# Queries, keys and four gate/up tiles of two token blocks as 2x2 block products of seven, in a layernorm, attention and SwiGLU kernel

## The chip, the cores and the metric

The kernel runs on one core of one Trainium2 chip. The metric is the device time of one execution in microseconds (us). The kernel before was run three times: median 1383.19, from 1383.1 to 1384.01. One further execution was profiled, and all views of the profile and the trace come from it.

## The reference, cut to what matters

```python
S, D, H, F = 2048, 512, 32, 1792           # rows of x, model width, heads (of 16), inner width
x  = A_x                                   # B_x is not used; all of it is fp32
xn = layernorm(x)                          # no scale, no shift
q, k, v = split(xn @ wqkv)                 # wqkv 512 x 1536, 32 heads of 16
s  = concat(softmax(q k^T / 4) v) @ wo     # full attention, no mask
h  = silu(xn @ w_gate) * (xn @ w_up)       # 2048 x 1792
g  = silu(h @ w_down)
out = x + s * g
```

## The kernel before

**Arithmetic.** Nearly all products run as three passes of the format fp32r: each operand is cut into a high part (a cast to fp32r) and a low part (the rest, by a subtract), and high x high, high x low and low x high are added in PSUM. Names ending in h and l, or a pair of tiles of one kind (`wh`/`wl`, `guh`/`gul`, `xt_...` twice), are such high and low parts. Only the product of probabilities and values (L450) runs in plain fp32.

**Blocks.** The 2048 rows are four blocks (b = 0 to 3) of 512 tokens. `xt` holds the normalised rows of a block turned, features on partitions, as high and low part; there are two buffers, so block 2 writes over block 0's and block 3 over block 1's.

**The prologue** runs 48 slots, twelve for each block: four value tiles (`value_tile`) and eight feature tiles (`feature_tile`, four of queries and four of keys, 128 features each). A slot is 12 full matmuls (L723 or L725: four chunks of 128 input features, three passes each). For blocks 0 and 1 the value tiles come first, for blocks 2 and 3 last. Behind the matmuls of a feature tile ScalarE takes the square (L778) and the high part (L779), VectorE the low part (L780), SyncE's queue stores both to `q_d` or `k_d`, and VectorE keeps the elementwise maximum of the squares in `top` (L784). A value tile is copied to `vt` and stored to `v_d` (L788), by GpSimd's queue for blocks 0 to 2.

The work between slots is set by a table of steps, `step(at, late, ...)`: at slot `at`, ahead of (0) or behind (1) its tile. `columns_of(b, ...)` places a block's rows: the load of x, its statistics and rates, a transpose of these (`spread_mr`), their way through DRAM (`mr_d`) into `wide_mr`, a tile with each token's mean and rate on all partitions (`load_mr`, L679, on GpSimd's DMA queue); then VectorE subtracts and multiplies each chunk in place (L667, `raw_x<-raw_x,wide_mr`), ScalarE casts it to the high part, VectorE makes the low part (also L667, `xt<-raw_x,xt`), and `store_x` (L658) stores the block's `xt` to `xt_d`, also on GpSimd's queue. The gate and down products of later blocks read `xt_d` into `fx` again; block 0's `fx` is copied directly (L819).

After the last feature tile the squares are summed by head and give a bound on all scores. Where it is small enough (`flag`), one common shift is used in place of each row's maximum; `tc.If` branches on it (L884, L887), and with these data the general way behind the branch isn't taken.

**The attention** runs 32 units (eight groups of four heads, four blocks of queries), each over 16 tiles of 128 keys. `plan()` cuts each unit into blocks of 2 to 6 key tiles, 102 blocks in all, by a search over costs. A block has two slots for each key tile, each with two score matmuls (L979, two heads side by side in the halves of the array), whose exponentials ScalarE makes from PSUM (L982 for two banks at once, L989 for one); the value matmuls of the block before stand behind the first key tile (L450). Where `SHARED` names slots of a block, VectorE copies one PSUM bank out (L986), and ScalarE exponentiates that copy at the end of the block (L999). L999 runs 354 times.

**The fill.** The rest of the plan says how many steps of other work follow each slot, so that TensorE has work while ScalarE makes exponentials. A step is a pair of matmuls on the two halves of the array (`both`, L244), which add into two banks. The steps come from a queue: `ffn(b)` for b = 0 to 3 in turn, each with inner tiles in two halves of seven; a half is seven gate units of 24 steps (gate and up together; their weights are cut by `split_gu`, L205 and L206) and four down units of 21 steps. `th` is the tanh of silu, `ga` the gated tile, `hh` its high and low part, `wd` those of w_down's tile, `facc` the sum of the first half of a block. Behind them comes the output projection, `project_out`, in part in the last units. The first 24 of these steps stand before the branch:

```python
                    fill(3 * DC)
                    fast = nc.values_load(flag, min_val=0, max_val=1)
```

Two value tiles' matmuls, the last slots of the prologue, are queued behind the reading of the flag as well, as the order below shows. L410 and L442, named in the prediction, are the closing sums of the output (GpSimd and VectorE); L579 is 11 matmuls of zeros at the very start, L639 the transposes of block 0's rows, L1034 the last products.

## Time and profile before

| | us |
|---|---|
| median of three runs | 1383.19 (1383.1 to 1384.01) |
| span of the profiled execution | 1381.3 |
| TensorE, matmuls busy | 1374.6 |
| TensorE, weight loads busy (beside matmuls) | 868.4 |
| ScalarE busy | 1157.9 |
| VectorE busy | 780.3 |
| GpSimd busy | 105.2 |
| DMA | 156.29 MB in 132900 packets |

The profile lists no time of the profiled execution but its span, which lies 1.9 us below the median of the other three runs. Busy times of different engines overlap. Half-height matmuls run in pairs, so the sum of their durations is more than the time that they fill, and a group of them reads 0.39 us for one while a pair takes 0.23.

### The profile page before, as it was taken

What the parts mean: (1) busy time and instruction counts of PE and PEld (TensorE: products, weight loads), DVE (VectorE), ACT (ScalarE), POOL (GpSimd) and SP (SyncE); (2) the same over time, 40 slices, a digit from 0 to 9 for tenths busy, and PEclk for the clock granted to TensorE, in tenths of its full rate; (3) what the DMA queues carried; (4) which work ended last, traced back from release to release, by engine and by line L of the source; (5) the groups of instructions that cost most, each with busy time, mean ns of one, the idle gap of its engine ahead of it and who ended that gap; (6) DMA issues with size and microseconds to landing.
All of it is one profiled execution on the core that took longest, in us unless ns stands there. A gap on an engine that the chain in (4) does not pass through costs nothing.

```text
span 1381.3 us, 27646 instructions
## 1 busy us (share of the span) xinstructions
PE 1374.6 (100%) x11152; PEld 868.4 (63%) x11152; DVE 780.3 (56%) x1255; ACT 1157.9 (84%) x1944; POOL 105.2 (8%) x148
## 2 busy tenths in 40 slices
PE   9999999999999999999999999999999999999998
PEld 7887666666655665665556656566556556656565
DVE  7674465356555663565465644565466445655656
ACT  6753689888988888899998998888989888899875
POOL 4300100000010000000010000000100000000142
PEclk9999999999999999999999999999999999999999
DMA  9799531134553511133814402257323312234652
GB/s 302 256 353 283 140 93 43 43 78 97 123 116 82 135 44 36 51 98 87 175 49 110 112 13 51 74 128 153 82 70 89 99 28 54 60 87 137 217 191 84
DMA packets 132900, 156.29 MB, mean 113 GB/s; under 512 B 13481, under 2 KB 83137, under 8 KB 131998
## 3 DMA queue, kind: packets, MB, share of 16 engines
q1 hardware_dynamic: 124974, 128.03, 36.0%
q0 software_dynamic: 7312, 25.89, 5.5%
q8 instruction: 89, 1.46, 0.5%
q10 hardware_dynamic: 480, 0.54, 0.1%
q14 instruction: 45, 0.37, 0.1%
HBM read 112.18 MB, written 40.12 MB: 110 GB/s over the span
## 4 chain that ended last, share of the span: by engine, by line
PE 89%; DVE 0%; DVEq 0%; issue 0%
PE acc L450 33%; PE bankx L244 29%; PE score L979 10%; PE single L979 8%; PE banky L244 7%; PE spare L979 1%; PE spare L1034 0%; PE banky L1034 0%; PE single L1034 0%; DVE guh L205 0%; DVE y L1041 0%; PE score L1034 0%; DVE y L1047 0%; DVEq L1094 0%; DVEq L205 0%
## 5 line engine op out<-in xcount | busy, mean ns | idle before, releaser
L450 PE MATMUL acc<-pr,vst 128*17 128x512 f32 x4096 | 459.3, 593 | 0.0
L989 ACT ACTIVATE pr<-single 128x512 f32<-128x512 f32 x762 | 429.5, 605 | 17.1 <-PE single L979 0.5
L982 ACT ACTIVATE pr<-score 128x1024 f32<-128x1024 f32 x318 | 328.1, 1032 | 87.1 <-PE score L979 84.3
L450 PEld LDWEIGHTS acc<-pr,vst 128*17 128x17 f32 x4096 | 115.5, 97 | 279.5 <-issue 275.2
L244 PE MATMUL banky<-fx,guh 64*128 64x512 f32 x896 | 291.0, 392 | 0.0
L244 PE MATMUL bankx<-fx,guh 64*128 64x512 f32 x896 | 290.6, 391 | 0.1
L986 DVE COPY pr<-spare 128x512 f32<-128x512 f32 x194 | 134.2, 692 | 182.7 <-PE spare L979 168.3
L979 PE MATMUL score<-qst,kst 50*128 50x512 f32 x830 | 219.0, 417 | 0.0
L979 PE MATMUL single<-qst,kst 50*128 50x512 f32 x922 | 212.7, 398 | 0.0
L244 PE MATMUL bankx<-wd,hh 64*128 64x512 f32 x672 | 196.0, 391 | 0.0
L244 PE MATMUL banky<-wd,hh 64*128 64x512 f32 x672 | 196.0, 391 | 0.0
L999 ACT ACTIVATE pr<-pr 128x512 f32<-128x512 f32 x354 | 193.4, 642 | 0.0
L244 PEld LDWEIGHTS bankx<-fx,guh 64*128 64x128 f32 x896 | 166.8, 186 | 21.0 <-DVE guh L205 0.5
L244 PE MATMUL bankx<-fx,gul 64*128 64x512 f32 x448 | 175.5, 392 | 0.0
L244 PE MATMUL banky<-fx,gul 64*128 64x512 f32 x448 | 175.5, 392 | 0.0
L979 PEld LDWEIGHTS score<-qst,kst 50*128 50x128 f32 x830 | 98.9, 183 | 112.4 <-ACT pr L989 69.0
L244 PEld LDWEIGHTS banky<-fx,guh 64*128 64x128 f32 x896 | 166.9, 186 | 0.7
L989 ACT ACTIVATE pr<-score 128x512 f32<-128x512 f32 x194 | 116.9, 603 | 35.5 <-PE spare L979 28.0
L986 DVE COPY pr<-single 128x512 f32<-128x512 f32 x160 | 110.5, 691 | 59.6 <-PE single L979 44.6
L244 PEld LDWEIGHTS bankx<-wd,hh 64*128 64x128 f32 x672 | 125.1, 186 | 16.4
L979 PEld LDWEIGHTS single<-qst,kst 50*128 50x128 f32 x922 | 115.0, 184 | 23.1 <-ACT pr L989 7.6
L244 PEld LDWEIGHTS banky<-wd,hh 64*128 64x128 f32 x672 | 125.1, 186 | 6.8
(195 smaller groups left out, 1690.1 us busy)
## 6 DMA issues: line engine op xcount, KB each, us to landing
gur<-in_B_w_gate_dram SPq DMA_DIRECT2D x56, 256.0 KB
gur<-in_B_w_up_dram SPq DMA_DIRECT2D x56, 256.0 KB
wdr<-in_B_w_down_dram SPq DMA_DIRECT2D x56, 256.0 KB
kst<-k_d SPq DMA_DIRECT2D x192, 64.0 KB
qst<-q_d SPq DMA_DIRECT2D x192, 64.0 KB
fx<-xt_d SPq DMA_DIRECT2D x24, 512.0 KB
q_d<-parts SPq DMA_DIRECT2D x16, 512.0 KB
k_d<-parts SPq DMA_DIRECT2D x16, 512.0 KB
```

The source lines that it names most:

```text
L244: mm(bank, lhs[h], rhs[h], start=start, stop=stop)
L450: mm(acc[h * 32:h * 32 + DH + 1], v[:, kt % CT, h * (DH + 1):(h + 1) * (DH + 1)], probs[2 * i + h // 2][:, h % 2], start=kt == 0, stop=kt ...
L979: mm(banked[h], k[r, j, kc * P:(kc + 1) * P], q[r, j], start=True, stop=True)
L982: exps.append(act(pr, both_banks, AF.Exp, scale=0.25))
L986: dve.tensor_copy(pr[:, h], banked[h])
L989: exps.append(act(pr[:, h], banked[h], AF.Exp, scale=0.25))
L999: exps.append(act(part, part, AF.Exp, scale=0.25))
```

## The change

**Seven products.** Queries and keys of blocks 2 and 3, and four of the 14 inner tiles of gate and up (`AHEAD`) for the same blocks, are computed in the prologue as eight jobs. A job takes two 128-wide tiles of weights (a query or key pair, or up and gate of one inner tile) against the two blocks of tokens, and reads them as a 2x2 product of blocks, split in the halves of the 512 input features: seven products in place of eight, by sums of weights and sums of rows. The 16 feature tiles of blocks 2 and 3 leave the slots, so that 32 slots are left: 12, 12, 4 and 4. Behind slot 31 come the jobs (q/k pair 0, pair 2, tile 0, pair 1, tile 1, pair 3, tile 7, tile 8), each of 7 x 6 full matmuls (L963).

A job's banks: the first and third product add up in one bank, which ScalarE copies after the first (`m1`, L972); VectorE adds the second to it (`w`, L974), and the fifth to that (`u3`, L988); `c12` (L999) and `c21` (L1005) are made by VectorE from the sixth and seventh, `c22` by GpSimd from `u3` and `m5`, ScalarE's copy of the fourth. The rows' sums are made once, from slot 26 on (`split_turn`, L908, cuts them in parts `twh`/`twl` that lie where weights were); the weights' sums on GpSimd (`sums`, L913 to L916), cut by `whole_of` and `summed_of` (L923 to L938) during the job before. Behind a q/k job's four results come square, high part, low part, store and maximum as before, with c22's low part on GpSimd; a gate/up job makes tanh and products `g1`, `g2` and stores them to `h_d`.

**Block 3 comes 8 slots earlier**, since eight feature tiles have gone ahead of it. Its rows are loaded into `facc` (called `xin`) and not `raw_x`, where GpSimd's sums now go.

**The branch.** The flag is made during the last job, and read behind it; no fill steps stand before the branch, and no value tile behind the reading.

**The FFN** runs by halves over `SEQUENCE`: half 0 of blocks 0, 2, 3, half 1 of blocks 0, 2, 3, 1, and half 0 of block 1, so that w_down's half is loaded three times and not eight. The sums of a first half of blocks 2 and 3 wait in `p_d`. The gated tiles made ahead come back from `h_d` into `hh` (`load_hidden`) and are cut by `split_hidden`. Gate steps fall from 56 units to 48.

**The plan** has new costs and 106 blocks, `SHARED` new entries (such copies rise from 354 to 422), and the value matmuls of a block take its tiles with shared slots last.

```diff
+AHEAD = (0, 1, 7, 8)
+    for b, grp in ((0, 0), (2, 0), (3, 0), (0, 1), (2, 1), (3, 1), (1, 1), (1, 0)):
...
-    short = lambda k, n: 60 if (k, n) in SHARED else 250 * max(0, 6 * (k - 1) - n)
+    short = lambda k, n: WAIT[k] + (65 if k == 4 else 160) * max(0, ENOUGH[k] - n)
...
+    def load_hidden(b, grp):
+        for f in AHEAD:
+            if b > 1 and GROUPS[grp].start <= f < GROUPS[grp].stop:
+                hidden.append(f - GROUPS[grp].start)
+                sp.dma_start(hh[:, hidden[-1], 1].bitcast(F32), h_d[b - 2, f])
...
-        u, tiles, probs = item
-        for i, kt in enumerate(tiles):
+        u, tiles, probs, order = item
+        for at, i in enumerate(order):
...
-    columns_of(2, raw_x, raw_x, (4, 11, 7, 9, 13, 13, 19, (1, 2, 3, 3)))
-    columns_of(3, xin, raw_x, (18, 24, 23, 25, 27, 27, 31, (1, 2, 3, 3)))
+    columns_of(2, raw_x, raw_x, (4, 11, 7, 9, 13, 13, 19, ((0, 0, 1), (1, 1, 2), (2, 2, 3), (3, 3, 3))))
+    columns_of(3, xin, xin, (14, 18, 16, 18, 20, 22, 24, ((0, 0, 1), (0, 1, 2), (1, 1, 2), (1, 2, 3))))
...
+        def split_turn(i, src):
+            t = turns_x[i] = [pc.tile([P, 2, TB], F32R, tag=f"{n}{i}", name=f"t{n}{i}") for n in ("wh", "wl")]
+            nc.scalar.copy(t[0], src)
+            dve.tensor_sub(t[1], src, t[0].bitcast(F32))
+
+        def sums(i):
+            s = raw_x.rearrange("p (i c) t -> p i (c t)", i=2)[:, i % 2].rearrange("p (i f) -> p i f", i=4)
+            raw = raws[i]
+            pool.tensor_add(s[:, 0], raw[:, 0], raw[:, 1])
+            pool.tensor_sub(s[:, 1], s[:, 0], raw[:, 2])
+            pool.tensor_sub(s[:, 2], raw[:, 2], raw[:, 0])
+            pool.tensor_sub(s[:, 3], raw[:, 3], s[:, 1])
...
+            if more:
+                sums(i + 1)
+            product(bank[0], whole[1], b11, True, False)
+            nc.scalar.copy(m1, bank[0])
+            product(bank[1], summed[1], t2, True, True)
+            dve.tensor_add(w, bank[1], m1)
+            if more:
+                whole_of(i + 1)
+            product(bank[0], whole[2], b21, False, True)
...
+                feature_out(2 * f, 2, bank[0], False)
+            product(bank[2], summed[0], t1, True, False)
+            nc.scalar.copy(m5, bank[2])
+            if between:
+                between()
+            product(bank[3], summed[2], t3, True, False)
+            dve.tensor_add(u3, bank[3], w)
+            pool.tensor_add(c22, u3, m5)
+            if more:
+                summed_of(i + 1)
...
+            product(bank[2], summed[3], b22, False, True)
+            dve.tensor_add(c12, bank[2], w)
...
+                feature_out(2 * f, 3, c12, False)
+            product(bank[3], whole[0], t4, False, True)
+            dve.tensor_add(c21, bank[3], w)
...
+                feature_out(2 * f + 1, 3, c22, True)
+                feature_out(2 * f + 1, 2, c21, False)
+
+        lower_x, upper_x = xin[:, :2], xin[:, 2:]
+        b11, b21 = ([xt[0][j][:, 2 * h:2 * h + 2].bitcast(F32) for j in range(2)] for h in range(2))
+        step(26, 1, dve.tensor_sub, wide_mr, upper_x, lower_x)
+        for j in range(2):
+            step(27, j, dve.tensor_sub, lower_x, lower_x, b11[j])
+        step(28, 0, dve.tensor_sub, upper_x, upper_x, lower_x)
+        step(28, 1, split_turn, 0, upper_x)
+        step(29, 0, split_turn, 1, lower_x)
+        step(29, 1, split_turn, 2, wide_mr)
+        step(30, 0, dve.tensor_sub, wide_mr, b21[0], upper_x)
+        step(30, 0, dve.tensor_add, wide_mr, wide_mr, b21[1])
+        step(30, 1, split_turn, 3, wide_mr)
+        step(26, 1, sums, 0)
...
-                    fill(3 * DC)
-                    fast = nc.values_load(flag, min_val=0, max_val=1)
...
+        for i in range(len(jobs)):
+            strassen(i, {6: bound, 7: spread_shift}.get(i))
+        load_wd(0, 0)
+        fast = nc.values_load(flag, min_val=0, max_val=1)
```

In the new program the stores of `store_x` are L719, `load_mr` is L740, the chunks' work L728, a feature tile's maximum L847, the flag L1098 and the branch L1100.

GpSimd's queue from block 1's store of values on, before (in these rows, `xt_169` and `xt_170` are block 2's, `xt_171` and `xt_172` block 3's high and low parts):

```order
L788 DMA v_d<-vt 128x8x272
L658 DMA xt_d<-xt_169 128x2048
L658 DMA xt_d<-xt_170 128x2048
L679 DMA wide_mr<-mr_d 128x1024
L658 DMA xt_d<-xt_171 128x2048
L658 DMA xt_d<-xt_172 128x2048
```

The same place in the new program (block 2 has `xt_177` and `xt_178`, block 3 `xt_179` and `xt_180`):

```order
L851 DMA v_d<-vt 128x8x272
L719 DMA xt_d<-xt_177 128x2048
L719 DMA xt_d<-xt_178 128x2048
L740 DMA wide_mr<-mr_d 128x1024
L913 TENSOR_TENSOR raw_x<-raw 128x256
L914 TENSOR_TENSOR raw_x<-raw_x,raw 128x256
L915 TENSOR_TENSOR raw_x<-raw 128x256
L916 TENSOR_TENSOR raw_x<-raw,raw_x 128x256
L719 DMA xt_d<-xt_179 128x2048
```

The order of the block's two stores and the load of wide_mr is the same; what moved is the block's norm behind that load, from slot 31 to slot 24, and job 0's sums now stand between the load and block 3's stores.

VectorE at block 3's rows, before; the chunks' subtracts and multiplies stand between low parts and maxima of feature tiles:

```order
L667 TENSOR_TENSOR raw_x<-raw_x,wide_mr 128x512 x2
L780 TENSOR_TENSOR parts<-ps,parts 128x512
L784 TENSOR_TENSOR top_163<-top_163,sq 128x512
L667 TENSOR_TENSOR raw_x<-raw_x,wide_mr 128x512 x2
L667 TENSOR_TENSOR xt_172<-raw_x,xt_171 128x512
```

VectorE at block 3's rows in the new program, up to the low parts of the first two sums of rows:

```order
L728 TENSOR_TENSOR facc<-facc,wide_mr 128x512 x8
L728 TENSOR_TENSOR xt_180<-facc,xt_179 128x512
L1050 MEMSET acc 128x512
L728 TENSOR_TENSOR xt_180<-facc,xt_179 128x512 x2
L728 TENSOR_TENSOR wide_mr<-facc 128x1024
L728 TENSOR_TENSOR facc<-facc,xt_177 128x1024
L728 TENSOR_TENSOR xt_180<-facc,xt_179 128x512
L728 TENSOR_TENSOR facc<-facc,xt_178 128x1024
L728 TENSOR_TENSOR facc<-facc 128x1024
L908 TENSOR_TENSOR twl_971<-facc,twh_970 128x1024
L908 TENSOR_TENSOR twl_975<-facc,twh_974 128x1024
```

All eight subtracts and multiplies of the block now stand in a row, with the sums of rows among the last low parts; behind the rows shown come another low part, the two operands of `t4` with theirs, and the first job's weights (L931 three times, 256 wide, and L938).

TensorE at the branch, before; 24 matmuls of two value tiles stand between the flag and the branch (the first three and the last two are shown):

```order
L884 TENSOR_LOAD flag
L725 MATMUL ps<-vh,xt_171 128x512
L725 MATMUL ps<-vh,xt_172 128x512
L725 MATMUL ps<-vl,xt_171 128x512
...
L725 MATMUL extra<-vh,xt_172 128x512
L725 MATMUL extra<-vl,xt_171 128x512
L887 COMPARE_AND_BRANCH
```

TensorE at the branch in the new program:

```order
L963 MATMUL ps<-twh_1021,odd 128x512
L963 MATMUL ps<-twl_1022,odd 128x512
L963 MATMUL ps<-twh_1021,odd 128x512 x2
L1098 TENSOR_LOAD flag
L1100 COMPARE_AND_BRANCH
```

The flag is now read behind the last job's last matmul, and the branch follows at once.

More of the change, by code (lines that the diff above doesn't have):

```diff
@@ L488, in tile_block @@
     u0 = units - NB + 1
-    queue = [[None, ffn(b), NF * 3 * (DC + NT)] for b in range(NB)]
+    queue = [[None, ffn(), sum(3 * (DC if u[0] == "gate" else FG) for u in SEQUENCE)]]
     queue += [[None, project_out(NB - 1, DT - 1), EARLY * 3 * (DT - 1)]]
@@ L495, in tile_block @@
     given = 0
-    now = -1
+    now = 0
     def fill(n):
@@ new lines, in summed_of, with feature_out @@
+        def summed_of(i):
+            t = [two.tile([P, 4, 2 * P], F32R, tag=tag, name="part") for tag in ("guh", "gul")]
+            src = weights[i][0]
+            nc.scalar.copy(t[0], src)
+            dve.tensor_sub(t[1], src, t[0].bitcast(F32))
+            weights[i].append([(t[0][:, k], t[1][:, k]) for k in range(4)])
+        def feature_out(m, b, src, pooled):
+            parts = p3.tile([P, 2, TB], F32R, tag="parts", name="parts")
+            sq = p5.tile([P, TB], BF, tag="sq", name="sq")
+            act(sq, src, AF.Square)
+            nc.scalar.copy(parts[:, 0], src)
+            (pool if pooled else dve).tensor_sub(parts[:, 1], src, parts[:, 0].bitcast(F32))
+            dst = (q_d if m < 4 else k_d)[:, (m % 4) * P:(m % 4 + 1) * P, b * TB:(b + 1) * TB]
+            sp.dma_start(dst.rearrange("s f t -> f s t"), parts.bitcast(F32))
+            dve.tensor_max(top[m], top[m], sq)
@@ L1007, in tile_block @@
                     coming.clear()
-            prev = u, tiles, probs
+            prev = u, tiles, probs, sorted(range(size), key=lambda i: max(0, *(n if n in shared else 0 for n in (2 * i, 2 * i + 1))))
             if now == begin[u] + (not u) and u + 1 < units:
```

361 lines of the change are left out of this document (237 added, 124 removed), and 15 rows, old and new, of the table SHARED.

## The prediction

> **What bounds the kernel now.** I read the page first, then the busy time of the two stages (the prologue up to the branch at 151 us, the attention behind it), then TensorE's timeline in a steady stretch.
>
> ```profile
> span 1381.3 us, 27646 instructions
> PE 89%; DVE 0%; DVEq 0%; issue 0%
> ```
>
> The chain that ended last is TensorE for 89% of the span, and no other engine has 1%.
>
> ```profile
> 0.00:151.00 151.00, 149.02 (x672) 117.95 (x674) 90.94 (x199) 81.16 (x141) 31.10 (x38) 1.00 0.89 285
> 151.00:1369.00 1218.00, 1218.00 (x10452) 744.92 (x10452) 681.38 (x1039) 1075.96 (x1802) 72.82 (x109) 1.00 0.37 92
> 1369.00:1381.30 12.30, 7.61 (x34) 5.49 (x30) 7.96 (x18) 0.81 (x2) 1.29 (x1) 0.96 0.25 95
> ```
>
> Columns: TensorE, weight load, VectorE, ScalarE, GpSimd, granted clock, DMA share. In both large stages TensorE never rests; ScalarE is at 88% of the attention, VectorE at 60% of the prologue.
>
> ```profile
> 262.31 5.34 PE L450 MATMUL acc<-pr,vst 128*17 128x512 f32 x48
> 267.59 0.50 PE L979 MATMUL score<-qst,kst 50*128 50x512 f32 x2
> 267.92 0.40 PE L244 MATMUL bankx<-wd,hh 64*128 64x512 f32 x1
> ...
> 274.00 0.40 PE L979 MATMUL score<-qst,kst 50*128 50x512 f32 x2
> ```
>
> From 267.92 to 274.00 lie 26 steps (a step is a pair of half-height matmuls side by side): 0.233 us each. The values of six key tiles take 267.59 - 262.31 = 5.28, or 0.88 a tile. The stage has 10452 - 4096 (values, L450) matmuls in pairs, 3178 steps: 3178 x 0.233 + 512 x 0.88 = 1191 of 1218 us; the other 27 are 0.26 for each of 102 blocks. So a step that leaves this stage is worth 0.233 us as long as ScalarE keeps up.
>
> ```profile
> 118.81 0.60 ACT L778 ACTIVATE sq<-ps 128x512 bf16<-128x512 f32 x1 [1.72 <-issue]
> 121.61 0.60 ACT L778 ACTIVATE sq<-ps 128x512 bf16<-128x512 f32 x1 [1.72 <-issue]
> 76.58 0.63 PE L723 MATMUL ps<-xt,wh 128*128 128x512 f32 x2
> ```
>
> A prologue slot (12 full matmuls) takes 2.80 us, again 0.233 a matmul; 76.58 is the start of slot 24, where the programs part.
>
> **The change: TensorE's work.** Eight gate units of 24 steps leave the attention, but 24 steps that stood before the branch now stand behind it: 168 steps x 0.233 = -39.1 us. Four blocks more at 0.26: +1.0. In the prologue 16 feature slots (192 matmuls) and those 24 steps go and eight jobs of 7 x 6 matmuls come: +120 x 0.233 = +28.0. Without any wait the sum is -10.1 us. Everything else is whether the other engines keep TensorE fed in a prologue that now asks far more of them.
>
> **Block 3's rows come late.** Block 3 must be normalised by slot 28 (it was slot 36), and the load of its rates (wide_mr) has moved from behind nothing to behind both stores of block 2 on GpSimd's queue.
>
> ```profile
> 54.53 1.07 POOL L658 DMA_DIRECT2D xt_d<-xt  x2
> 55.59 0.91 POOL L788 DMA_DIRECT2D v_d<-vt  x1
> 78.35 0.53 POOL L658 DMA_DIRECT2D xt_d<-xt  x1 [1.20 <-DVE xt L667]
> ```
>
> ```profile
> L679 POOL DMA_DIRECT2D wide_mr<-mr_d x3: 536/570/571, 27.8 to 91.7; - x3
> ...
> DMA to landing us min/median/max: 4.9/6.0/6.8
> ```
>
> ```profile
> L658 POOL DMA_DIRECT2D xt_d<-xt x1: 534/534/534, 78.4 to 78.4; - x1
> ...
> DMA to landing us min/median/max: 10.1/10.1/10.1
> ```
>
> ```profile
> L788 POOL DMA_DIRECT2D v_d<-vt x1: 911/911/911, 55.6 to 55.6; - x1
> ...
> DMA to landing us min/median/max: 13.9/13.9/13.9
> ```
>
> These are the times from issue to landing of all three wide_mr loads, of the xt_d store issued at 78.35 alone, and of the v_d store issued at 55.59 behind two xt_d stores. The load can be issued at 78.35 + 0.53 = 78.9. Lower end: it lands as the fastest one, 83.8. Upper end: stores of one queue land one after the other, as v_d did, 69.5; then the load comes after 78.35 + 10.1 = 88.5 and needs some 2.5 for its 512 KB, 91.0. I take 87, the middle, since the same k_d stores and other loads run beside it in both programs.
>
> VectorE then has a chain that nothing shortens. Its prices:
>
> ```profile
> 74.22 1.41 DVE L667 TENSOR_TENSOR raw_x<-raw_x,wide_mr 128x512 f32<-128x512 f32 x2
> 75.83 0.69 DVE L780 TENSOR_TENSOR parts<-ps,parts 128x512 fp32r<-128x512 f32 x1 [0.20 <-ACT parts L779]
> 76.44 0.41 DVE L784 TENSOR_TENSOR top<-top,sq 128x512 bf16<-128x512 bf16 x1
> L206 DVE TENSOR_TENSOR gul<-gur,guh 128x1024 fp32r<-128x1024 f32 x56 | 68.6, 1225 | 2.1
> L819 ACT CAST fx<-xt 64x1024 fp32r<-64x1024 f32 x16 | 16.8, 1048 | 0.3
> L779 ACT CAST parts<-ps 128x512 fp32r<-128x512 f32 x32 | 18.6, 582 | 3.6 <-DMA q_d<-parts 3.0 <-DMA k_d<-parts 0.6
> ```
>
> Instructions follow each other 0.08 sooner than they last (75.83 to 76.44), so 512 wide is 0.61, 1024 wide 1.15. Until the low part of block 3's last chunk: four subtract-multiply pairs 4 x 1.35, three low parts 1.8, memset 0.5, two 1024-wide 2.3, the last low part 0.7: 10.7. Slot 28 needs that part for its eleventh matmul, due at 76.6 + 11.2 + 2.3 = 90.1; it gets it at 87 + 10.7 = 97.7. Then two 1024-wide operations (2.3), a ScalarE cast (1.05), three low parts (3.45), two operands (2.3), a cast (1.05), the fourth low part (1.15), and two 256-wide (0.7, estimated from the 512- and 1024-wide rows), with 0.3 of hand-overs: 12.3 more. So the first job starts 23 after the landing, at 110, where slot 31 without waits would have ended at 76.6 + 8 x 2.80 = 99.0. That is +11. The sums of job 1 run on GpSimd in the same stretch:
>
> ```profile
> 1350.76 1.28 POOL L410 TENSOR_TENSOR pair<-facc,pair 128x512 f32<-128x512 f32 x1 [2.45 <-DVE facc L409]
> 1352.62 2.15 DVE L442 TENSOR_TENSOR facc<-facc,on 128x512 f32<-128x512 f32 x1
> 1352.92 1.30 POOL L410 TENSOR_TENSOR pair<-facc,pair 128x512 f32<-128x512 f32 x1
> ```
>
> A two-input subtract on VectorE ended 0.55 after GpSimd's did, 1.46 longer than its kind: they exclude each other. Four 256-wide sums at 0.65 (half of 1.3) hold VectorE for 0 to 2.6; I take 1. **Term: +12, ends 7.8 (landing at 83.8) and 17.6 (91.0 and 2.6).**
>
> **The jobs wait for each other's tail.** A job is 42 x 0.233 = 9.8 us of TensorE. In a q/k job VectorE has ten 512-wide operations or fewer (w, u3, c12, c21, three low parts: 4.3), four maxima (1.3), 0.9 and 1.15 for the next job's weights: 7.7, but at the end it stands in a row with ScalarE. c12's bank is complete 8.4 into the job; c12 is out at 9.2, Square and cast (1.1) 10.3, low part and maximum 11.3, c21 12.0, its Square and cast 13.1. Only then comes ScalarE's copy of the next job's m1, done at 13.7. The next job's third product adds to that bank and is due at 9.8 + 2.8 = 12.6: it waits about 1.4. Four q/k jobs each have a follower: 5.6. The gate/up jobs have no Square, cast and maximum behind c12, and cost nothing beside the 9.8. GpSimd's share (four sums, c22, one low part: 2.6 + 1.3 + 1.3 = 5.2 of every 9.8 us) excludes VectorE's two-input work; from nothing to 1.5 a q/k job, I take 2.9 in all. **Term: +8.5, ends 4 and 12.** The table load of tanh (1.28 in either program) falls into a gate/up job, where ScalarE rests.
>
> **The branch.**
>
> ```profile
> L884 PEldq TENSOR_LOAD <-flag x1: 490/490/490, 142.3 to 142.3; - x1
> L887 PEldq COMPARE_BRANCH  x1: 3434/3434/3434, 146.4 to 146.4; - x1
> ```
>
> Before, 24 value matmuls were queued between reading the flag and the branch, and the 3.4 us of it passed under them. Now nothing stands between, and TensorE's sequencer can read the flag only once the last product's wait is over, with some 2 us of matmuls left: 0 (were the branch only waiting for queued work) to 2.3. I take +1.
>
> **The attention.** ScalarE keeps 1076 us of work, less 8 tanh and more single-bank exponentials, in some 1180 us: 91%. New (3,9) and (4,15) blocks and new shared slots may cost 0.06 a block (+6) or save 0.04 (-4); I take +0.5. The round trips of h_d and p_d, three more loads of fx, and 35 fewer weight splits on VectorE count nothing: DMA is at 37%, and 84 down steps (about 47 us) lie between a load of fx and its use; without that cover each fx load would cost 10 us. A split of a reloaded gate tile that comes before its DMA would hold VectorE's line for some us; the +6 covers it.
>
> **Sum:** -10.1 + 12 + 8.5 + 1 + 0.5 = +11.9: a span of 1393.2. The profiled execution's span lies 1.9 below the median of the runs, 1383.19, so I forecast 1395.1.
>
> **A rule on the clock.**
>
> ```profile
> 1.07 4.41 PE L579 MATMUL extra<-busy 128*128 128x128 f32 x22 [1.07 <-DVE ind L586]
> 13.50 0.60 PE L639 MATMUL acc<-ident,xn 128*128 128x128 f32 x4
> ```
>
> The first 22 small passes took 4.41 us; at the spacing of the later four (0.11) they take 2.6: a cold start costs 1.8. At the end, too, the granted clock sinks (0.96 over the last 12.3 us). The waits at slot 28 and before the first job are gaps of 3 to 4 us: if the clock falls in both, 2 x 1.8 = +3.6 more. The Trainium skill (TensorE: Matmul & The Clock Gate, Part 1) says that an idle window of about 3.4 us halves TensorE's clock and that as long a busy one restores it; by that rule the sum would be +15.5. The rows show the cold start, but no gap inside the kernel, so the forecast leaves it out.
>
> **Rivals.**
> 1. As forecast, and the clock falls in both gaps: 1395.1 + 3.6 = 1398.7. For it: cold start; against it: the gap at slot 28 is broken by a few matmuls.
> 2. The load isn't held behind the stores and lands at 83.8, GpSimd holds nothing up, the branch is free: 7.8 + 5.6 + 0.5 - 10.1 = +3.8, 1387.0. For it: the other loads of wide_mr took 4.9 to 6.8. Against it: v_d's 13.9.
> 3. Faster: VectorE's chain isn't what TensorE waits for, because two-input operations with ScalarE's casts beside them run at 0.7 for 1024 elements and not at 1.15. The chain shrinks from 23 to about 15, the first job starts at 102, the tails close: 3 + 0.5 of stalls, -6.6, 1376.6 (1380.6 if the tails keep their lower end of 4). It decides once all stalls together are under 10.1 - 2.8 = 7.3, so the first job must start by about 105. Against it: 56 such subtracts with a mean of 1225 ns.
> 4. The change does not do what it says: no; the step counts are fixed by the code, and -39 in the attention holds unless ScalarE binds.
>
> **How the numbers follow.** Forecast 0.55 (its own range 1389 to 1400), rival 1 0.12, rival 2 0.17, rival 3 0.16. Less than 0.2% (2.8 us) is about what a measurement of this kernel can't tell from no change. Of rival 2, 0.10 is slower and 0.07 the same; of the forecast, 0.03 falls within the bound (stalls at several lower ends); rival 3 is faster. So faster 0.16, same 0.10, slower 0.52 + 0.12 + 0.10 = 0.74. The range reaches from the slower side of rival 3 to rival 1's upper side, 1379 to 1402.
>
> **What would show it.** TensorE idle from about 88 to 98 us with the first wait ended by VectorE's norm (L728), which itself waits for the DMA of wide_mr; the first L963 matmul at 107 to 114; a wait of 1 to 2.5 us at L963 in the jobs that follow a q/k job, ended by ScalarE's m1 (L972); the first score matmul near 200 (it was 151.4); from there to the end some 1193 us (it was 1230). The prediction is wrong if the first L963 matmul stands at or before 103, or if the attention stretch gets shorter by over 45 us or by under 30.

## The result, and the profile after

The changed kernel takes 1449.38 us (median of four runs, 1447.94 to 1451.09), the kernel before 1383.29 on the same chip: a ratio of 1.0478, with an interval from 1.0463 to 1.0493. Forecast were 1395.1 and a range to 1402. The direction was right; the loss is 66 us and not 12.

The page of the changed kernel, its span and the chain that ended last:

```profile
span 1447.5 us, 27367 instructions
PE 77%; DMA 6%; ACT 2%; DVE 1%; SPq 1%; POOL 0%; issue 0%; DVEq 0%; ACTq 0%
```

Before, TensorE alone had 89% of this chain and DMA did not appear. Now DMA has 6%, some 87 us in which the end hung on a transfer. Where it was waited for, by TensorE's waits over the whole span (engine, line, what was waited for; us in all, times, the longest):

```profile
PE score L1191 <- DMA kst<-k_d: 14.3, 1, 14.3
PE score L1191 <- POOL kst L177: 8.6, 1, 8.6
PE ps L787 <- ACT xt L728: 7.2, 1, 7.2
PE bankx L278 <- DVE y L334: 7.1, 1, 7.1
PE ps L963 <- ACT spots L972: 6.2, 4, 1.6
PE ps L787 <- DVE xt L728: 4.7, 3, 3.1
PE ps L963 <- ACT whole L930: 3.2, 1, 3.2
```

The kernel before has two waits in this view, 1.9 us in all:

```profile
PE extra L579 <- DVE ind L586: 1.1, 1, 1.1
PE acc L639 <- DVE xn L634: 0.8, 1, 0.8
```

Busy times by stage (columns as before: TensorE, weight load, VectorE, ScalarE, GpSimd, granted clock, DMA share, GB/s), cut at the first job, the last job's end, the first score and near the end:

```profile
0.00:117.90 117.90, 100.90 (x421) 78.42 (x421) 78.36 (x162) 66.41 (x113) 37.22 (x44) 0.96 0.88 284
117.90:205.60 87.70, 81.30 (x345) 63.57 (x345) 71.28 (x106) 46.20 (x79) 46.28 (x37) 0.98 0.57 169
205.60:217.30 11.70, 0.76 (x5) 0.33 (x5) 7.08 (x9) 0.63 (x1) 5.34 (x5) 0.70 0.32 92
217.30:1435.00 1217.70, 1193.52 (x10112) 693.92 (x10112) 658.69 (x1006) 1068.53 (x1777) 69.31 (x105) 0.99 0.41 98
```

Against the forecast:

| stage | forecast | measured |
|---|---|---|
| first job starts | 110 | 117.9 |
| eight jobs | 78.4 + 8.5 = 86.9 | 87.7 |
| last product to first score | 1 | 11.7, with two steps in it |
| first score to the end | 1193 | 1447.5 - 217.3 = 1230.2 |

The time of the jobs came out as forecast. The rows differ by 37 us in the attention, 11 at the branch, 8 ahead of the first job and 1 in the jobs, 57 in all. The spans differ by 54.3: the forecasts in this table add up to 1390.9 us, 2.3 less than the forecast span; 1 us of that is GpSimd's sums ahead of the first job.

**In the attention** TensorE stands still twice. SyncE's DMA queue around both places (SPq is the part of SyncE that issues its DMAs; start, time, what is issued; a row merges issues of one kind with the waits between them):

```profile
833.29 5.18 SPq L244 DMA_DIRECT2D fx<-xt_d  x8
838.84 20.36 SPq L318 DMA_DIRECT2D part<-p_d  x2
966.26 5.15 SPq L244 DMA_DIRECT2D fx<-xt_d  x8
971.57 14.00 SPq L186 DMA_DIRECT2D kst<-k_d  x6
```

A reload of fx is eight DMAs of 512 KB. At 838.84 the first sum that comes back from p_d stands behind it, at 971.57 the next group's keys. VectorE's closing sum of a down unit (L334) waited 14.05 for the first, and TensorE, whose banks it holds, 7.1; the score on the keys waited 14.3. The kernel before has three such reloads and TensorE waits for none; the changed one has six. Ahead of each, SyncE itself stands still until TensorE is done with the old fx, and what it would issue next stands behind that too (all six, the longest; 12.5 us of it ahead of 833.29 and 17.1 ahead of 966.26):

```profile
SPq L244 <- PE bankx L278: 94.7, 6, 17.1
```

**Behind each longer wait the granted clock is at half** (0.50 also from 982 to 994 at the keys, from 96 to 104 at block 3's rows and from 211 to 219 at the branch). The stretches around the first wait of the attention, and the step at which it ended:

```profile
854.00:856.00 2.00, 0.00 (x0) 0.00 (x0) 0.00 (x0) 0.00 (x0) 0.00 (x0) 0.83 1.05 197
856.00:858.00 2.00, 0.00 (x0) 0.00 (x0) 0.00 (x0) 0.00 (x0) 0.00 (x0) 0.50 0.28 55
862.00:864.00 2.00, 2.00 (x12) 1.60 (x10) 0.82 (x3) 1.08 (x2) 0.00 (x0) 0.50 0.73 222
866.00:868.00 2.00, 2.00 (x20) 1.66 (x18) 1.49 (x3) 1.38 (x2) 0.00 (x0) 1.00 0.00 0
858.88 0.79 PE L278 MATMUL bankx<-wd,hh 64*128 64x512 f32 x1 [7.10 <-DVE y L334]
```

TensorE stopped at 858.88 - 7.10 = 851.8; the mean of 0.83 says that the clock fell at about 855.3, 3.5 later. From 862 to 864 it ran 12 matmuls where the full clock gives 20. The Trainium skill (TensorE: Matmul & The Clock Gate, Part 1) gives about 3.4 us of idle time for the fall to half; these rows agree. At the other waits it took 3.3 to 4.4 us (last section).

**Ahead of the first job** the rows of block 3 came late, as forecast, and later still:

```profile
81.28 0.54 POOL L740 DMA_DIRECT2D wide_mr<-mr_d  x1
94.80 5.41 DVE L728 TENSOR_TENSOR facc<-facc,wide_mr 128x512 f32<-128x512 f32 x8 [13.04 <-DMA wide_mr<-mr_d]
117.91 1.14 PE L963 MATMUL ps<-xt,whole 128*128 128x512 f32 x2 [3.19 <-ACT whole L930]
```

The load was issued at 81.28 and landed at 94.8; from there to the first job lie 23.1 us, where the forecast had a chain of 23 and 1 more for GpSimd.

**At the branch** each engine has to pass on its own. The instruction that it runs behind the branch on the side taken, before and after, with the first score of each kernel:

```profile
L887 SPq EVENT_SEMAPHORE  x8: 17/17/17, 148.3 to 148.9; - x8
L887 DVEq EVENT_SEMAPHORE  x1: 21/21/21, 150.0 to 150.0; - x1
151.45 0.69 PE L979 MATMUL score<-qst,kst 50*128 50x512 f32 x2
```

```profile
209.15 1.49 SPq L229 DMA_DIRECT2D wdr<-in_B_w_down_dram  x1
L1100 SPq EVENT_SEMAPHORE  x8: 17/17/17, 214.4 to 216.9; - x8
L1100 DVEq EVENT_SEMAPHORE  x1: 21/21/21, 212.5 to 212.5; - x1
217.32 0.99 PE L1191 MATMUL score<-qst,kst 50*128 50x512 f32 x2 [8.59 <-POOL kst L177]
```

SyncE's eight stand for the eight semaphores of its loads and stores. In the program each waits until everything issued under its semaphore has landed and then raises it by what the side not taken would have added; the first score waits for those values. So the first score comes behind the last engine's pass: 0.4 us behind SyncE's, 216.9. The view names GpSimd's setting of kst as releaser, but in the program this matmul waits for no kst of that line; in the run with the reloads on GpSimd's queue, below, the same view names SyncE's pass:

```profile
PE score L1191 <- SPq L1100: 8.7, 1, 8.7
```

The landings themselves don't show as the limit here. The last load, w_down's, had landed by 212.4, when GpSimd started on what waited for it (by the view), the DMA share is 0.03 from 213 to 215, and yet the first of the eight stands at 214.4 and the last at 216.9. What shows is when SyncE gets there: it issues the two h_d stores (207.4 and 208.8, each when VectorE has made its tile) and w_down's load first, reads the flag at 210.7, branches at 211.6, and is through 5.3 us later.

### The profile page after: what moved, and what is told of

The parts are those of the page before. It is cut to its first block, busy times and chain, and to the rows that moved or that the text cites. A ratio compares the mean times of both kernels' runs of the same rounds, so it can differ in the third digit from the quotient of the medians.

```text
span 1447.5 us, 27367 instructions
## 1 busy us (share of the span) xinstructions
PE 1384.4 (96%) x10912; PEld 841.7 (58%) x10912; DVE 823.4 (57%) x1299; ACT 1182.6 (82%) x1971; POOL 159.4 (11%) x191
## 4 chain that ended last, share of the span: by engine, by line
PE 77%; DMA 6%; ACT 2%; DVE 1%; SPq 1%; POOL 0%; issue 0%; DVEq 0%; ACTq 0%
PE acc L511 28%; PE bankx L278 23%; PE score L1191 9%; PE single L1191 8%; PE banky L278 7%; DMA fx<-xt_d 2%; DMA qst<-q_d 1%; DMA part<-p_d 1%; DMA kst<-k_d 1%; PE ps L963 1%; PE spare L1191 1%; SPq L244 1%; ACT pr L1201 1%; ACT pr L1211 1%; ACT pr L1194 0%; POOL kst L177 0%
## 5 line engine op out<-in xcount | busy, mean ns | idle before, releaser
L1201 ACT ACTIVATE pr<-single 128x512 f32<-128x512 f32 x673 | 387.1, 607 | 20.4 <-PE single L1191 14.7
L1194 ACT ACTIVATE pr<-score 128x1024 f32<-128x1024 f32 x335 | 345.7, 1032 | 57.9 <-PE score L1191 46.1
L278 PE MATMUL bankx<-fx,guh 64*128 64x512 f32 x768 | 254.6, 393 | 2.4 <-DVE wide_mr L1009 2.4
L278 PE MATMUL banky<-fx,guh 64*128 64x512 f32 x768 | 254.3, 393 | 0.0
L1191 PE MATMUL score<-qst,kst 50*128 50x512 f32 x847 | 229.0, 419 | 24.8 <-DMA kst<-k_d 14.3
L1198 DVE COPY pr<-single 128x512 f32<-128x512 f32 x245 | 168.6, 688 | 123.8 <-PE single L1191 121.6
L1211 ACT ACTIVATE pr<-pr 128x512 f32<-128x512 f32 x422 | 232.0, 642 | 0.0
L278 PEld LDWEIGHTS bankx<-fx,guh 64*128 64x128 f32 x768 | 143.5, 187 | 20.6 <-DVE wide_mr L1009 2.8
L278 PE MATMUL bankx<-fx,gul 64*128 64x512 f32 x384 | 151.1, 393 | 0.0
L278 PE MATMUL banky<-fx,gul 64*128 64x512 f32 x384 | 151.0, 393 | 0.0
L278 PEld LDWEIGHTS banky<-fx,guh 64*128 64x128 f32 x768 | 143.6, 187 | 2.7
L278 PEld LDWEIGHTS bankx<-wd,hh 64*128 64x128 f32 x672 | 127.0, 190 | 21.4 <-DVE y L334 7.4
```

Of the source, the lines that this page charges most:

```text
L278: mm(bank, lhs[h], rhs[h], start=start, stop=stop)
L1191: mm(banked[h], k[r, j, kc * P:(kc + 1) * P], q[r, j], start=True, stop=True)
L1194: exps.append(act(pr, both_banks, AF.Exp, scale=0.25))
L1198: dve.tensor_copy(pr[:, h], banked[h])
L1201: exps.append(act(pr[:, h], banked[h], AF.Exp, scale=0.25))
L1211: exps.append(act(part, part, AF.Exp, scale=0.25))
```

## The experiments

All start from the changed kernel at 1449.4 us. The theory after the first look: (a) reloads of fx hold up SyncE's queue, (b) the branch waits for landings and slow engines, (c) block 3's rates stand behind block 2's stores, (d) a q/k job's outputs hold the next job's m1. The rival to all of them: the work itself (busier DMA engines, more blocks and copies, a ScalarE that doesn't keep up) costs the time, and the waits only show it. Without an interval, a time is a single run; the changed kernel's own four runs spread over 3.2 us, so a gain of 3 to 7 us is read from its stage in the trace and not from the total alone.

**Reloads on another queue.**

```diff
-                sp.dma_start(dst[u], xt_d[b, j, u * HALF:(u + 1) * HALF])
+                pool.dma_start(dst[u], xt_d[b, j, u * HALF:(u + 1) * HALF])
```

> The changed kernel, with the six reloads of fx (eight DMAs of 512 KB each) issued on GpSimd's queue in place of SyncE's; nothing else. Theory (the queue): in the attention TensorE stands still twice, 7.1 us for a sum that was to come back from p_d and 14.3 us for keys, because these small loads stand behind such a reload on SyncE's queue. On another queue they no longer do: both waits go, with the slow clock behind them (some 5 us), so the time falls from 1449 by 22 to 28, to 1421 to 1427. Rival (the DMA engines): the 4 MB of a reload fill all 16 engines for some 20 us whichever queue they come from, and small loads land as late as before: 1441 or more.

Measured: 1418.42, 31.0 less, a little beyond the theory's side. Both waits are gone. The attention's row:

```profile
216.10:1404.00 1187.90, 1186.99 (x10108) 692.10 (x10112) 658.89 (x1006) 1068.12 (x1777) 98.57 (x154) 1.00 0.42 101
```

The DMA share is 0.42, as before the edit (0.41): as much was moved, but TensorE ran 1187 of 1188 us, at a mean clock of 1.00. The rival falls. From the first score to the end it is 1416.6 - 216.1 = 1200.5 us and not 1230.2, so 29.7 of the 31 were won here; the first job also started 1.6 sooner. SyncE's and GpSimd's issues at the first place in this run:

```profile
816.71 25.96 SPq L318 DMA_DIRECT2D part<-p_d  x2
829.50 4.98 POOL L244 DMA_DIRECT2D fx<-xt_d  x8 [11.13 <-PE bankx L278]
```

The first sum from p_d is now issued 12.8 us ahead of the reload, and the keys of the second place at 945.4, 6.4 ahead of theirs: SyncE no longer stands until TensorE is done with fx. So this run alone can't tell that standing from the burst's transfer.

**The same reloads, same queue, in parts.**

```diff
-                sp.dma_start(dst[u], xt_d[b, j, u * HALF:(u + 1) * HALF])
+                to_load.append((dst[u], xt_d[b, j, u * HALF:(u + 1) * HALF]))
...
+                if to_load:        # at the end of the last gate unit and of three down units
+                    load_some()    # two of the eight
```

> The changed kernel, with each reload of fx still on SyncE's queue but in four parts of two DMAs (1 MB), one behind the last gate unit and one behind each of the next three down units. Theory (what stands behind a long reload waits for all of it): a part holds the queue for some 5 us and not 20, the sums from p_d and the keys come in time, and most of the 31 us that GpSimd's queue won are won here too: 1418 to 1428. Rival (GpSimd's queue helped because its transfers are served beside SyncE's, not because of the order): the same 4 MB on the same queue cost as much in parts, 1438 or more.

Measured: 1418.27, as much as from the other queue; 28.8 of the gain lie behind the first score (1416.3 - 214.9 = 1201.4 us). SyncE's queue at the first place:

```profile
828.47 1.23 SPq L250 DMA_DIRECT2D fx<-xt_d  x2
829.75 0.60 SPq L324 DMA_DIRECT2D part<-p_d  x1
830.40 1.17 SPq L250 DMA_DIRECT2D fx<-xt_d  x2
841.59 0.35 SPq L324 DMA_DIRECT2D part<-p_d  x1
```

The sum from p_d now stands behind two DMAs and not eight. SyncE still stands 12.5 and 17.1 us ahead of the two reloads, and that costs TensorE nothing. What counted was the length of what is ahead in the same queue, neither its owner nor the bytes. The Trainium skill (DMA: Bandwidth & Descriptors, Queues, rings and completion order) says that each engine takes turns between queues packet by packet. The gain from GpSimd's queue doesn't test that, as the small loads went out ahead of the bursts there, and the parts show that turns aren't needed when the burst is short.

**The FFN in the order before.**

```diff
-    for b, grp in ((0, 0), (2, 0), (3, 0), (0, 1), (2, 1), (3, 1), (1, 1), (1, 0)):
+    for b, grp in ((0, 0), (0, 1), (1, 0), (1, 1), (2, 0), (2, 1), (3, 0), (3, 1)):
...
-        if b > 1:
+        if False:
```

> The changed kernel with the FFN in the order of the kernel before: both halves of block 0, then of 1, 2 and 3; so three reloads of fx in place of six, w_down's halves loaded eight times, first halves of all blocks kept in place and no p_d. Products of seven, prologue and SHARED as in the changed kernel; the plan is worked out again from the same costs. Theory (the queue): the two waits of 7.1 and 14.3 us in the attention come from the order by halves alone; they go, with the slow clock behind them: 1421 to 1427. Rival (the plan: more blocks, 418 slots copied by VectorE, ScalarE behind): the stretch from the first score to the end keeps at least 20 of the 38 us that it has over the sum without waits, 1435 or more.

This kernel also leaves out the renewal of the seventh w_down tile in the halves of blocks 2 and 3 (a cast and a subtract on VectorE for each), so it doesn't compute the same, and it is used here for the waits alone. Measured: 1422.29, 27 less. With three reloads and no p_d the two waits are gone as well; so it is the order by halves that brought them; whether by the number of reloads, by p_d or by where the reloads fall, this run doesn't part.

**The branch.**

```diff
-        load_wd(0, 0)
         fast = nc.values_load(flag, min_val=0, max_val=1)
...
+        load_wd(0, 0)              # behind the branch
...
-                sp.dma_start(h_d[0, f], g1)
+                (sp if more else pool).dma_start(h_d[0, f], g1)    # and g2
```

> The changed kernel, with the first load of w_down moved behind the branch, and the two h_d stores of the last job on GpSimd's queue; nothing else. Theory (the drain): the side of the branch that is taken lets the attention go on only once every load and store on SyncE's queue has landed; the last h_d store and w_down's load were issued at 208.8 and 209.2 us and landed at 212.4, then some 4.6 us for the branch itself, so the first score came at 217.3. With the shift's loads (issued by 204.3) as the last ones, it comes at about 211: 1449 falls by 6 to 8. Rival (the fixed price): reading the flag and branching with nothing queued behind costs what it costs, 2 us or less are won.

Measured: 1444.85, 4.5 less: between both. The first score came at 212.2. SyncE branches at 205.3 and not at 211.6, but its pass still takes 6.4 us and ends at 211.7. So does VectorE's, since VectorE still makes g1 and g2 until 208.6 and needs 3.3 us from its last work ahead of the branch to its first behind it. One cause was removed and another stood 0.0 us behind it.

**Work ahead of the branch.**

```diff
-    first = [(4, ends[0])]
+    ends = [n - ends[0] for n in ends[1:]]
+    first = [(4, ends[0])]
...
+        fill(3 * DC)
         load_wd(0, 0)
         fast = nc.values_load(flag, min_val=0, max_val=1)
```

> The changed kernel, with the first gate unit (24 steps, 5.6 us of TensorE) run between the last job and the reading of the flag, as the kernel before has it; the plan is made for the rest. Theory (uncovered drain): the 11 us from the last product to the first score are the branch's own time; work in front of it covers what lies between, up to 5.6, and these steps leave the attention; TensorE is cold for a shorter time: 1449.4 falls by 5 to 8. Rival (moved along): since TensorE's sequencer reads the flag behind its queue, flag, branch and the landing of the last loads simply come 5.6 later: within 2 of 1449.4.

Measured: 1442.73, 6.7 less. From the end of the last product to the first score lie 11.1 us, 205.4 to 216.5 (11.7 before the edit), but 5.6 of them are TensorE's work now. The first job of this run also started 1.6 earlier than in the profile above (it varies from 115.3 to 117.9 over the six runs that leave its rows alone), so some 5 belong to the edit. That is cover, as forecast, and no shorter branch.

**Rates first.** The load of block 3's wide_mr ahead of block 2's stores:

```diff
-            for make in steps.pop((at, late), ()):
+            for make in sorted(steps.pop((at, late), ()), key=lambda m: m.func is store_x):
```

> The changed kernel, with the load of block 3's rates (wide_mr) ahead of block 2's two xt_d stores on GpSimd's queue. Theory (behind the stores): it can then be issued at about 78 and lands by 86, not 94.8; the first job starts at 107 to 110 and not 117.9, and the time falls by 8 to 11. Rival (the engines are full): with 386 GB/s moved from 85 to 90 us the load lands late from either place, and the first job starts at 114 or later; 4 us or less are won.

Measured: 1443.46, 5.9 less, though the first job started at 109.7, 8.2 sooner, as the theory said. Part of the gain was lost to the clock, from rows inside job 0:

```profile
113.00:115.00 2.00, 2.00 (x6) 1.54 (x5) 0.00 (x0) 1.32 (x2) 0.00 (x0) 0.50 1.11 326
115.00:117.00 2.00, 2.00 (x6) 1.59 (x5) 1.24 (x2) 0.00 (x0) 0.00 (x0) 0.50 0.77 179
```

The clock was at half for 6 us here, and the products of the eight jobs took 89.1 us (87.3 in the changed kernel).

**Rates in a tile of their own.** As above, and the load doesn't wait for block 2's norm:

```diff
+            rates_of[b] = two.tile([P, 2, TB], F32, tag="guh", name="wide_3") if b == 3 else wide_mr
+            pool.dma_start(rates_of[b], mr_d...)
```

> The changed kernel, with the rates of block 3 in a tile of their own (where weights were staged), loaded one slot sooner and ahead of block 2's stores, so that the load waits neither for the stores nor for block 2's norm. With the load only moved ahead of the stores the first job started 8 earlier, at 110. Theory (VectorE's chain of 23 us behind the landing): the chain starts when VectorE is through with block 2, at 82, and the first job at 105, 13 earlier than 117.9: 1449.4 falls by 9 to 13. Rival (the engines): weights, stores and keys fill the DMA engines from 76 to 90 us, the stretch of the jobs grows by what the start wins, and the gain stays under 7.

Measured: 1441.92, 7.5 less; the first job started at 111.4 and not at 105. The load was issued at 74.8 and landed in 6.4, as hoped. A new wait stood behind it, on ScalarE:

```profile
101.87 0.59 ACT L871 COPY vt<-ps 128x512 f32<-128x512 f32 x1 [12.48 <-DMA v_d<-vt]
```

ScalarE waited 12.5 us for a store of block 2's values, with the casts of the rows' sums queued behind.

**Late outputs of q/k jobs.**

```diff
-                feature_out(2 * f + 1, 3, c22, True)
-                feature_out(2 * f + 1, 2, c21, False)
+                late_outs.append(partial(feature_out, 2 * f + 1, 3, c22, True))   # made behind
+                late_outs.append(partial(feature_out, 2 * f + 1, 2, c21, False))  # the next job's m1
```

> The changed kernel, with the outputs of a q/k job's c22 and c21 (square, high part, low part, store, maximum) issued behind ScalarE's copy m1 of the next job, so that this copy no longer stands behind them. Theory (tails): the four waits of TensorE for m1 (L972, 1.5 us each, 6.2 in all) go, the time falls from 1449.4 by 5 to 7. Rival (work only moved): what is held back then delays the same job's later copies and the weights' parts, and less than 3 us are won.

Measured: 1445.74, 3.7 less, between both. The waits for m1 are gone; 2.3 us of waits for u3 (VectorE) and 1.0 for m5 (ScalarE) took their place. The jobs' products took 85.1 us in place of 87.3, so some 2.2 belong to the edit.

**A warm TensorE.**

```diff
+            for _ in range(0 if i else 13):
+                mm(bankx, xt[0][0][:, 0, :P], xt[0][0][:, 0], start=True, stop=True, skip_group_check=True)
             product(bank[0], whole[1], b11, True, False)
```

> The changed kernel, with 13 full matmuls more, whose result nothing reads, ahead of the first job's first product: they have all that they need and run in the 3.2 us in which TensorE waits there for the job's weights. Theory (the clock): the granted clock fell to 0.50 from about 118 to 121.5 because TensorE had stood still before; with work in the gap it stays at 1.00, the matmuls of job 0 follow each other every 0.23 us from the first, and job 0 ends 1.5 to 2 us sooner. Rival (something else slows job 0, loads of weights or PSUM): the spacing of 0.42 stays, or the 13 matmuls only come on top (+1 to +3).

Measured: 1446.07. The same stretches, first of the changed kernel, then of this one:

```profile
117.00:119.00 2.00, 1.09 (x2) 0.41 (x2) 1.73 (x3) 2.00 (x5) 0.00 (x0) 0.76 0.00 0
119.00:121.00 2.00, 1.82 (x5) 1.49 (x5) 1.64 (x3) 0.59 (x2) 0.00 (x0) 0.50 0.08 22
```

```profile
117.00:119.00 2.00, 2.00 (x10) 1.49 (x9) 1.04 (x1) 1.14 (x2) 0.00 (x0) 1.00 0.34 93
119.00:121.00 2.00, 2.00 (x11) 1.60 (x10) 1.56 (x2) 0.45 (x2) 0.00 (x0) 1.00 1.14 324
```

The clock stayed at 1.00, as the theory said; the jobs' products took 86.4 us and not 87.3. That 0.9 is this gap's cold start, half of what was expected, since job 0 also waits for weights meanwhile. The rest of the 3.3 us is the earlier start of this run (115.3).

**All of them in one** (reloads on GpSimd's queue, branch, own rates, late outputs, work ahead of the branch):

> All of them in one: fx reloads on GpSimd's queue, the first w_down load behind the branch and the last job's h_d stores on GpSimd's queue, rates of block 3 in a tile of their own, late outputs of q/k jobs, the first gate unit ahead of the branch. If the waits found are all there is, the gains add up: 31 + 9 (branch) + 11 + 6 = 57 below 1449.4, so 1389 to 1397, still over the 1383.3 of the kernel before, since the chain of 23 us behind block 3's rates stays 6 late and the attention keeps 6 to 9 over its sum. If a gain only moves a wait, 1400 or more.

Measured: 1403.97, ratio 1.0147 to the kernel before (1.0130 to 1.0164). Of the single gains' sum of 53.4 us (31.0 + 4.5 + 6.7 + 7.5 + 3.7) 45.4 arrived; the theory wanted 1397 or less, its rival 1400 or more. The branch's two remedies overlap: from the end of the last product to the first score 11.2 us are left, 5.6 of them work. Its rows:

```profile
L1117 DVEq EVENT_SEMAPHORE  x1: 21/21/21, 204.9 to 204.9; - x1
205.14 0.99 PE L1209 MATMUL score<-qst,kst 50*128 50x512 f32 x2 [2.13 <-POOL kst L178]
```

Now VectorE is the last engine through, since the gate unit's end runs on it until 201.9, and the first score follows by 0.2.

**Block 2's values off the keys.** The first loads of keys, queries and values behind the third job:

```diff
-                if b == 2 and n in (1, 3):
-                    load_k(0, n // 2)
...
+            if i == 2:
+                for c in range(2):
+                    load_k(0, c)
+                    load_v(0, c)
+                load_q(0)
```

> All remedies in one as before (1404.0), and the first loads of keys, queries and values moved from slots 25 to 30 to behind the third job, so that block 2's v_d stores no longer stand behind them on SyncE's queue. In the version before, ScalarE's copy of a value tile waited 8.0 us for such a store, at 97.6, and with it the casts of the rows' sums. Theory (that queue is the next wait): the first job starts at 103 to 105 and not at 108, the time falls by 3 to 6, to 1398 to 1401. Rival (VectorE's chain is as long anyway): under 2 us are won. Neither is under the 1383.3 of the kernel before.

Measured: 1404.59 (ratio 1.0153, 1.0136 to 1.0170): nothing won, the first job started at 107.95 and not at 108.1. ScalarE's wait for the store is gone, and VectorE's chain ends when it did. The rival holds.

**One step less ahead of the branch.**

```diff
-        fill(3 * DC)
+        fill(3 * DC - 1)
```

> All remedies in one as in the run of 1404.0, with 23 steps of the first gate unit ahead of the branch and not 24, so that the unit's end (tanh on ScalarE, two products on VectorE) comes behind the branch. Theory (the last engine through the branch decides): in the run of 1404.0 the first score, at 205.14, came 0.2 behind VectorE's own pass of the branch (204.9), which came 3 us after its last work ahead of it, the unit's end (until 201.9). Without that end VectorE is through at about 202, and the first score comes at 202.3: the time falls by 2 to 4, to 1400 to 1402. Rival (SyncE's loads or GpSimd's setting of kst decide): the first score stays at 205, 1403 to 1405.

Measured: 1713.58, ratio 1.2392 (1.2357 to 1.2427). The branch did what the theory said:

```profile
L1117 DVEq EVENT_SEMAPHORE  x1: 21/21/21, 201.1 to 201.1; - x1
```

VectorE passed it at 201.1 and not 204.9, though the first score still came at 204.3, behind the unit's end, which had only been moved. But every unit now ended one step into the next block and not at a block's end:

```profile
PE bankx L279 <- DVE ga L311: 101.1, 48, 2.4
```

At a block's end the value matmuls stand between a unit's last step and the next unit's first; one step later the two meet, and TensorE waits 2.1 us for the banks, 48 times, with a clock that falls again and again (0.94 over the run). What this edit shows of the branch is therefore read from that row alone.

## Why the prediction was wrong

**The attention: this step failed.** It said that the round trips and three more loads of fx "count nothing: DMA is at 37%, and 84 down steps (about 47 us) lie between a load of fx and its use". Both facts hold, and nobody waited for fx. I priced the load's own user and not what stands behind it on SyncE's queue: the sums from p_d and the keys. It cost about 29 us of the 37 that the attention lies over its forecast (29.7 with the reloads on another queue, 28.8 in parts, single runs; that the two totals agree within 0.2 is partly luck). Of these, 21.4 are the two waits and some 5 the clock at half behind them (858.9 to 865.6 and 991.6 to 995.2, at half the rate); the other 2 to 3 aren't placed. The mean DMA share could not show it: the share is 1.05 in the rows around 855 and 0.41 on average. The step count held: with the reloads out of the way the stretch is 1200.5 us, where the steps gave 1229.8 - 39.1 + 1.0 = 1191.7 without waits. Of the 9 left, some 2 are the clock at half behind the branch; the rest lies spread over the blocks, and whether it is ScalarE (90% busy) was not tried.

**The branch: the term was mis-sized**, 0 to 2.3 us against 11. I took TensorE's own reading and branching as the price. The two h_d stores and w_down's load that the change puts ahead of the branch, and VectorE's end of the last job, decide, and SyncE, VectorE and TensorE each need about 3 us from the branch to the next instruction (SyncE 211.6 to 214.4). In the kernel before, SyncE and VectorE were through at 148.9 and 150.0, under two value tiles of work.

**Block 3's rows: right in kind, too small.** The chain measured 23.1 against 23 and 1 for GpSimd, but that it came so near is partly luck. Its first part, to the last low part, was right (10.8 against 10.7). Of the second, the fourth low part and the weights' low parts (1.9 us of the chain) end behind the start of the first job; in their place stand VectorE's 1024-wide work beside GpSimd's sums (1.65 for one subtract and 2.91 for two, where one alone took 1.22) and ScalarE's casts of the weights (0.7 us). With the rates first, the same chain took 25.5 us (84.2 to 109.7). The landing was 94.8, outside my 83.8 to 91.0. I wrote that the load had moved behind block 2's stores; the order is the same in both programs, and what changed is that the load is issued 0.5 us behind the second store and not 13 us (78.35 and 91.7 in the kernel before). The load was issued 2.4 later than I had it, as the second store waits for VectorE's last low part, and landed 13.5 behind its issue, where my upper case had 12.1. The experiment that moved the load ahead of the stores won the 8.2 us at the first job.

**The jobs' tails: the wait was right, the sum partly luck.** Forecast 8.5, of which 5.6 for four followers at about 1.4 and 2.9 for GpSimd; measured 87.7 - 78.4 = 9.3 with 6.2 of waits for m1 in four jobs. TensorE's other waits in this stretch are 0.2, so the 2.9 don't show; what fills their place is mostly job 0, whose first product took 3.2 us at the lower clock where 1.4 is its work.

**The clock** was rival 1, with 3.6 us for two gaps. It fell as described there, but behind the branch and both waits of the attention too. What one gap costs isn't fixed: against the 86.4 us of the jobs' products with a warm TensorE, 0.9 in the changed kernel, and 2.7 where job 0 ran at half clock for 6 us (89.1, in the run with the rates first).

**The range** came from terms that I had written down; three more loads at "nothing" had no upper end in it, and that was the step worth 29.

## What to carry to other kernels

For every long transfer that a change adds, list what the same queue issues in the next 20 us and when each is due, and whether the issuing engine stands still ahead of the transfer until its buffer is free; issue the burst in parts between the small loads, or on another queue. Ahead of a branch, ask of every engine when it gets there, the one that issues the DMAs included, and leave work for TensorE behind the reading of the flag. Where a plan lets units of work end at block ends, a step more or less ahead of it shifts all of them.

## What the runs showed of the hardware that was not expected

From the branch instruction to the first one behind it SyncE took 2.6 to 3.6 us in all kernels and VectorE 2.9 to 3.6; TensorE's branch instruction itself lasted 3.4 to 4.1. GpSimd took only 0.2 to 0.5 where no work of its own lay between (the kernel before, branch, all in one). The first score followed the last pass by 0.2 to 0.5 us in four kernels: 216.9 to 217.3 (changed), 211.7 to 212.2 (branch), 216.2 to 216.5 (work ahead), 204.9 to 205.1 (all in one).

The granted clock fell 3.3 to 4.4 us after TensorE had stopped, by the mean of the stretch in which it fell: 3.5 at the first wait of the attention, 4.3 at the keys (stopped at 977.3; mean 0.90 from 980 to 982), 4.4 at block 3's rows (89.7; 0.53 from 94 to 96) and 3.3 ahead of job 0 (114.7; 0.76 from 117 to 119), there even though TensorE was at work again from 117.9. At the branch it fell at 210.2 (0.80 from 209 to 211), 1.5 us after two steps that ran alone from 208.0 to 208.7: so short a piece of work in the gap did not keep it up.
